# Dividing the rows of one weight matrix among the DMA engines in another way

## The chip, the cores and the metric

The kernel runs on one core of a Trainium2 chip. A core has five engines that work side by side and meet at semaphores: TensorE (PE, matmuls into PSUM; PEld are its weight loads), VectorE (DVE), ScalarE (ACT), GpSimd (POOL) and SyncE (SP), which here issues most of the transfers. Sixteen DMA engines move data between HBM and SBUF, whose 128 partitions are the rows of every tile. The metric is the device time of one execution in microseconds, lower is better.

## What is computed

One decode step for four sequences: an attention block with a KV cache and a gMLP block, both on the same layer-normed input, and their sum with the input itself.

```
def _A_ref(x, k_cache, v_cache, wq, wo):          # B=4, H=32, Sk=4096, Dh=128, D=640
    q = (x @ wq) -> [B, H, 1, Dh]
    p = softmax(q . k_cache * Dh ** -0.5)
    return (p . v_cache) -> [B, 1, H * Dh] @ wo

def _B_ref(x, w_in, w_sp, b_sp, w_out):           # F=1728, Fh=864
    z = gelu(x @ w_in)
    z1, z2 = z[..., :Fh], layernorm(z[..., Fh:])
    g = w_sp * z2 + b_sp
    return (z1 * g) @ w_out

xn = layernorm(x)
out = x + _A_ref(xn, ...) + _B_ref(xn, ...)
```

The K and V caches are 134 MB each in bf16, nearly all of the 282 MB that the kernel reads. The matrix of this study, `w_out`, has 864 rows of 640 values, 1,280 bytes a row, 1.1 MB.

## The kernel before

**Order of the work.** SP's queue loads `wq`, `w_in`, most of `w_out`, and then K and V units in the order of `seq`: four K units, then V unit, K unit in turn. A unit is 8 heads of one sequence, 8.4 MB, 65,536 bytes in each partition. `place` gives each unit two of the five slots of the SBUF tile `kv`; a unit is loaded by `load_unit` (L181) when what lay in its slots has been used. After the last V unit `load_wo` (L189) loads the last three quarters of `wo`, the very last one in five pieces. Meanwhile DVE transposes the K units (L425), PE makes scores (L436) and weighted sums of V (L509), and at the end PE projects with `wo` (L552) and the result goes out (L617, L620).

**The gMLP** lies at the start, while K unit 0 is loaded. The 864 values of z are laid out in SBUF as chunks of up to 128, one value a partition, so that each chunk can be multiplied with as many rows of `w_out`, one row a partition. There are FC = FA + FR chunks: FA = 3 full ones, whose rows lie in `w_out` (in `kv`), and FR more that use only some partitions, whose rows lie in `w_rest`, a view of `w_words`. Partitions that hold no row there are zero (the memset at L128). The matmuls of L338, L339 and L343 make z, ACT applies GELU (L349, L357, L360), POOL and DVE do the layer norm and the gate on 32 x FC wide tiles (L371 to L390), and L403 multiplies with `w_out`, two matmuls a chunk, into `proj`. `w_words` later takes the transposed K units, so L425 can start after L403.

**How `w_out` is divided.** The first 384 rows go to all 128 partitions, three rows each, by SP's queue (L126, L127). The other 480 rows go by the three pieces of `PC`. An entry (p0, p1, n, k) says: partitions p0 to p1, n rows in each, and the source seen as k blocks of rows (`load_piece`, L133), so that k DMA engines move it, one block each. In the trace the first piece has landings on five engines and the second on three of these five. Both go by SP's queue, the third by GpSimd's, on two other engines. `walk` (L141) is a small load by GpSimd's queue on seven engines ahead of the third piece; its data is not used, and the third piece is issued after it.

```
PC = ((0, 20, 10, 5), (32, 44, 12, 3), (60, 68, 17, 2))
return eng.dma_start(out=w_rest[p0:p1, 0:n].rearrange("p c n -> p (c n)"),
                     in_=B_w_out[f_at[t]:f_at[t + 1], :].rearrange("(r i c) n -> i r (c n)", i=k, c=n))
```

So the five engines of the first piece move 4 partitions of 10 rows each, the three of the second 4 partitions of 12 rows, the two of the third 4 partitions of 17 rows.

**Semaphores of transfers.** The transfers of SP's and ACT's queues use eight semaphores in turn. A transfer whose semaphore was used before waits until that earlier transfer has landed, besides waiting for its data and its place.

Of the kernel before, what the change touches and what calls it, by code (L numbers as in the profile page):

```python
# [16 lines left out]
def kernel(  # L17
# [19 lines left out]
    nc = tc.nc  # L37
    P = 128
# [3 lines left out]
    DC = D // P  # L42
# [9 lines left out]
    NG = H // HG  # L52
# [2 lines left out]
    F2 = B_w_in.shape[1]  # L55
    Fh = F2 // 2
    FA = 3
    FR = 17
    nf = FA * P

    PC = ((0, 20, 10, 5), (32, 44, 12, 3), (60, 68, 17, 2))
    f_at = [nf]
    for p0, p1, n, _ in PC:
        f_at.append(f_at[-1] + (p1 - p0) * n)
    assert Fh == f_at[-1]
    FC = FA + FR
    NOUT = A_wo.shape[1]
# [18 lines left out]
    def misc_ps(shape, dtype):  # L86
        misc_ctr[0] += 1
        return ps_m.tile(shape, dtype, tag="misc", name=f"misc{misc_ctr[0]}")
# [5 lines left out]
    n_p = (2 * TC + 1) * 16  # L94
    w_words = const.tile([P, max(2 * NKT + n_p, FR * NOUT // 2)], F32, name="w_words")
    kT_t = w_words[:, 0:2 * NKT].rearrange("p (i n) -> p i n", i=2)
    pT_t = w_words[:, 2 * NKT:2 * NKT + n_p].bitcast(BF16).rearrange("p (j r) -> p j r", r=32)

    def at_slot(i, n, off=0):
        return kv[:, i * SL + off:i * SL + off + n]  # L100
# [22 lines left out]

    w_out = at_slot(2, FA * NOUT, n_in).rearrange("p (c n) -> p c n", c=FA)

    nc.sync.dma_start(out=w_out[:, 0:2], in_=B_w_out[0:2 * P, :].rearrange("(p c) n -> p c n", p=P))  # L126
    nc.sync.dma_start(out=w_out[:, 2:3], in_=B_w_out[2 * P:nf, :].rearrange("(p c) n -> p c n", p=P))  # L127
    nc.vector.memset(w_words[:, 0:FR * NOUT // 2], 0.0)  # L128
    w_rest = w_words[:, 0:FR * NOUT // 2].bitcast(BF16).rearrange("p (c n) -> p c n", c=FR)

    def load_piece(eng, t):
        p0, p1, n, k = PC[t]
        return eng.dma_start(out=w_rest[p0:p1, 0:n].rearrange("p c n -> p (c n)"),  # L133
                             in_=B_w_out[f_at[t]:f_at[t + 1], :].rearrange("(r i c) n -> i r (c n)", i=k, c=n))
# [39 lines left out]
    def load_unit(item):  # L174
        key, u = item
        g, b = divmod(u, B)
        cache = A_k_cache if key == "k" else A_v_cache
        src = cache[b, g * HG:(g + 1) * HG].rearrange("e (m t) d -> (e m) (t d)", t=T)
        c = cuts.get(item, (0, T))
        for t0, t1 in zip(c[:-1], c[1:]):  # L180
            nc.sync.dma_start(out=unit(item, t0, t1), in_=src[:, t0 * Dh:t1 * Dh])  # L181
# [5 lines left out]
    def load_wo(g, c_cuts=(0, HG)):  # L187
        for c0, c1 in zip(c_cuts[:-1], c_cuts[1:]):
            nc.sync.dma_start(out=wo_t[g][:, c0:c1, :], in_=wo_q[g][:, c0:c1, :])  # L189
# [30 lines left out]
    xnT = const.tile([P, DC, 32], BF16)  # L220
# [43 lines left out]
    for q in range(4):  # L264
        nc.gpsimd.tensor_copy(out=SelE[32 * q:32 * q + 32, :, q % 2, :],
                              in_=b8[32 * q:32 * q + 32, 8:8 + HP, None].to_broadcast((32, HP, P // HG)))
# [10 lines left out]
                          in_=ident_f[:].rearrange("p (q x c) -> p q x c", q=2, c=C2))  # L277
# [12 lines left out]
    for hf in range(NH):  # L290
        nc.tensor.matmul(proj[0:32, 0:NO2], lhsT=ident_bf[:XR, 1 - hf:33 - hf],
                         rhs=x_bf[:, hf * NO2:(hf + 1) * NO2], start=(hf == 0), stop=False)
# [4 lines left out]
    for hf in range(2):  # L297
        for c in range(DC):
            for j in range(NG):
                n0 = j * HG * Dh + hf * 512  # L300
                nc.tensor.matmul(q4_ps[32 * j:32 * j + 32, hf * 512:hf * 512 + 512], lhsT=xnT[:, c, :],  # L301
                                 rhs=wq[:, c, n0:n0 + 512], start=(c == 0), stop=(c == DC - 1))
# [14 lines left out]
    w_z = w_in.rearrange("p c (a f) -> p c a f", a=2)  # L317
    z_ps = misc_ps([P, 2, FA, 32], F32)
# [3 lines left out]
    z_in = [[], [], [], []]  # L322
    for t, (p0, p1, n, k) in enumerate(PC):
        src = w_z[:, :, :, f_at[t]:f_at[t + 1]]
        for q in range(p0 // 32, (p1 - 1) // 32 + 1):
# [5 lines left out]
                src_q = src  # L331
            z_in[q].append((t, x0 - 32 * q, x1 - 32 * q, src_q))
    z_of = [[sum((x1 - x0) * PC[t][2] for t, x0, x1, _ in z[:m]) for m in range(len(z) + 1)] for z in z_in]
    w_z2 = w_z[:, :, :, 0:2 * P].rearrange("p c a (q j i) -> p c q a i j", q=4, j=32)
    w_z1 = w_z[:, :, :, 2 * P:nf].rearrange("p c a (q j) -> p c q a j", q=4)
    for c in range(DC):
        for q in range(4):
            nc.tensor.matmul(z_ps[32 * q:32 * q + 32, :, 0:2], lhsT=xnT[:, c, :], rhs=w_z2[:, c, q], start=(c == 0), stop=False)  # L338
            nc.tensor.matmul(z_ps[32 * q:32 * q + 32, :, 2], lhsT=xnT[:, c, :], rhs=w_z1[:, c, q], start=False,  # L339
                             stop=(c == DC - 1))  # L340
        for q in range(4):
            for m, (_, _, _, src) in enumerate(z_in[q]):
                nc.tensor.matmul(zr_ps[32 * q:32 * q + 32, :, z_of[q][m]:z_of[q][m + 1]], lhsT=xnT[:, c, :], rhs=src[:, c],  # L343
                                 start=(c == 0 and m == 0), stop=(c == DC - 1 and m == len(z_in[q]) - 1))
# [5 lines left out]
    for q in range(4):  # L350
        rows = slice(32 * q, 32 * q + 32)
        for m, (t, x0, x1, _) in enumerate(z_in[q]):
            p0, p1, n, k = PC[t]
            z = zr_ps[rows, :, z_of[q][m]:z_of[q][m + 1]]
# [3 lines left out]
            else:  # L358
                for a in range(2):
                    nc.scalar.activation(out=dst[:, a].rearrange("p c (i r) -> p c i r", i=k),  # L360
                                         in_=z[:, a].rearrange("p (r i c) -> p c i r", i=k, c=n), func=ACT.Gelu_apprx_tanh)
# [36 lines left out]
    for f0 in range(0, FC, 4):  # L398
        for hf in range(NH):
            for fc in range(f0, min(f0 + 4, FC)):  # L400
# [3 lines left out]
                                 rhs=(w_out[:, fc] if fc < FA else w_rest[:, fc - FA])[:, hf * NO2:(hf + 1) * NO2],  # L404
                                 start=(fc == 1 and hf == 0), stop=False)
# [11 lines left out]
    def emit_K(u, k):  # L417

        g, b = divmod(u, B)
        hh = first.get(u, 0) ^ (k // 4)  # L420
        qp, kh = k // 2 % 2, k % 2
        t0 = 2 * TC * (2 * hh + qp)
        kw = unit(("k", u), t0, t0 + 2 * TC).bitcast(F32).rearrange("p (t w) -> p t w", w=KW)[:, :, 32 * kh:32 * kh + 32]
        kT = kT_t[:, k % 2]
        nc.vector.transpose(kT.rearrange("p (t r) -> p t r", r=32), kw)  # L425
        if ("S", g) not in state:
            S_new = ps_s.tile([P, 2, TC, M], F32, tag="S", name="S")
            state[("S", g)] = S_new
        S_ps = state[("S", g)]
        kb = kT.bitcast(BF16).rearrange("p (i t e m w) -> p i t e m w", i=2, e=NE, m=M, w=2)  # L430
        w0 = 8 - (b * C2 + hh)
        for w in range(2):
            for i in range(2):
                for e in range(NE):
                    q = 2 * qp + e
                    nc.tensor.matmul(S_ps[32 * q:32 * q + 32, i], lhsT=QZ[:, b, 2 * kh + w, e, w0:w0 + 32],  # L436
                                     rhs=kb[:, i, :, e, :, w], start=(b == 0 and k < 4 and kh == 0 and w == 0),
                                     stop=(b == B - 1 and k >= 4 and kh == 1 and w == 1))
# [89 lines left out]
    def emit_sel(g):  # L528

        ox = misc_ps([P, B, P // HG, HG], F32)  # L530
        nc.tensor.matmul(ox[:].rearrange("p b q c -> p (b q c)"), lhsT=SelX[:].rearrange("p h q -> p (h q)"),  # L531
                         rhs=state["R"][:].rearrange("p b d -> p (b d)"), start=True, stop=True)
        om = ppool.tile([P, B, P // HG, HG], F32, tag="p", name="om")
        nc.vector.tensor_tensor(out=om[:], in0=ox[:], in1=MkQ[:, None, :, None].to_broadcast((P, B, P // HG, HG)), op=ALU.mult)
        state[("om", g)] = om
# [19 lines left out]
    def emit_proj(g, h2=range(2), close=False):  # L555
        for h in h2:
            for hf in range(NH):
                for c in range(4 * h, 4 * h + 4):
                    o_mul(proj[32 * (c % 2):32 * (c % 2) + 32], g, c, hf, hf * NO2, (hf + 1) * NO2, False,
                          close and c == HG - 1 and hf == NH - 1)  # L560

    fill_qz(0)
    for i, item in enumerate(seq):
        if i + 1 < len(seq):
            key, u = seq[i + 1]
            load_unit(seq[i + 1])
            if key == "k" and u == 2 * B - 1:
                load_wo(u // B - 1)
        else:
            load_wo(NG - 3)  # L570
            load_wo(NG - 2)
            load_wo(NG - 1, (0, 2, 4, 6, 7, 8))
        key, u = item
        g, b = divmod(u, B)
        if key == "k":
            done = b == B - 1 and g > 0
            for k in range(8):
                emit_K(u, k)
                if done and k == 1:
                    emit_sel(g - 1)  # L580
                if done and k == 2:
                    emit_oT(g - 1)
                if done and k == 5 and g == 1:
                    emit_proj(g - 1)
            if b == B - 1:
                if g < NG - 1:
                    fill_qz(g + 1)
                softmax(g)
        else:
            emit_V(u)  # L590
# [58 lines left out]
```

## Time and profile before

| | us |
|---|---|
| median of 3 runs | 663.35 (663.31 to 664.25) |
| profiled execution | 663.36 |
| its span, first to last instruction | 661.6 |
| PE, DVE, ACT, POOL busy | 281.7, 377.3, 73.9, 70.3 |
| HBM read | 282.25 MB, 427 GB/s over the span |
| `w_in` landed | 23.89 |
| gMLP: last matmul of L403 ends | about 43.9 |
| K unit 0 landed, first transpose starts | 45.52, 45.74 |
| last piece of `wo` landed | 658.46 |

The profile's page gives each engine's busy time, the span in 40 slices with the share of the DMA engines that is busy, the chain of work that ended last, and groups of instructions with what they waited for. The chain is read backwards from the last instruction; "DMA kv<-in_A_k_cache_dram" in it is time in which the next step waited for that transfer. A line such as "SPq L181 <- X: 9.6, 1, 9.6" says that SP's queue at L181 waited 9.6 us in total for X, once, 9.6 us at the longest. Besides the page, the trace has every DMA packet with its start, duration and size, and the events by which transfers raise their semaphores.

### The profile page before, as it was taken

To read this page: it belongs to the slowest core of one execution; us is meant where nothing else is said; L and a number is where in the kernel's file an instruction comes from. 1 tells how busy PE (TensorE), PEld (TensorE's weight loads), DVE (VectorE), ACT (ScalarE), POOL (GpSimd) and SP (SyncE) were. 2 spreads that over 40 slices of the span, in tenths; PEclk is the share of its full clock that TensorE was granted. 3 is DMA by queue.
4 is the path that set the end of the run, shared out by engine and by line. 5 is a ranking of instruction groups with operands and counts; after the bars stand their busy time and mean duration, and the time that the engine had idled before them with its cause. 6 is when DMAs were issued, how large, how long until landed. Compare 5 with 4: busy or idle time off the path is not lost.

```text
span 661.6 us, 5513 instructions
## 1 busy us (share of the span) xinstructions
PE 281.7 (43%) x2293; PEld 106.9 (16%) x2293; DVE 377.3 (57%) x307; ACT 73.9 (11%) x143; POOL 70.3 (11%) x138
## 2 busy tenths in 40 slices
PE   0445555437052455334435075532606245652236
PEld 0221111112011121111112021110202112120012
DVE  4329989766191758718346196864629175971112
ACT  0300000330100000340200000070110000043200
POOL 3620000030200000130300000030020000003300
PEclk9868879778687697677759677875867778666779
DMA  8999999999999999999999999999999999999997
GB/s 367 458 421 440 425 436 445 436 421 440 421 436 437 444 405 436 441 441 436 433 420 428 437 422 445 442 425 432 432 433 432 433 440 411 446 432 429 423 423 286
DMA packets 7276, 282.60 MB, mean 427 GB/s; under 512 B 929, under 2 KB 1324, under 8 KB 1836
## 3 DMA queue, kind: packets, MB, share of 16 engines
q1 hardware_dynamic: 7112, 282.07, 98.9%
q8 instruction: 18, 0.29, 0.2%
q0 software_dynamic: 112, 0.18, 0.1%
q14 instruction: 6, 0.05, 0.0%
q10 hardware_dynamic: 28, 0.01, 0.0%
HBM read 282.25 MB, written 0.01 MB: 427 GB/s over the span
## 4 chain that ended last, share of the span: by engine, by line
DMA 74%; DVE 12%; issue 11%; PE 2%; ACT 0%; SPq 0%; DVEq 0%; ACTq 0%
DMA kv<-in_A_k_cache_dram 63%; DVE w_words L425 11%; DMA kv<-in_A_v_cache_dram 5%; DMA kv<-in_A_wo_dram 3%; DMA kv<-in_A_wq_dram 3%; PE O L509 1%; DVE w_words L491 0%; PE S L436 0%; DVE Zb L469 0%; DVE m L443 0%; PE last L552 0%; ACT p_bf L485 0%; SPq L189 0%; PE proj L552 0%; PE misc L447 0%
## 5 line engine op out<-in xcount | busy, mean ns | idle before, releaser
L425 DVE STREAM_TRANSPOSE w_words<-kv 128x2048 f32<-128x2048 f32 x128 | 282.8, 2275 | 127.2 <-DMA kv<-in_A_k_cache_dram 127.2
L436 PE MATMUL S<-w_words,QZ 128*32 128x512 bf16 x1024 | 183.3, 490 | 262.5 <-DVE w_words L425 262.5
L436 PEld LDWEIGHTS <-QZ 128*32 128x32 bf16 x1024 | 59.2, 110 | 384.3 <-issue 318.1
L509 PE MATMUL O<-kv,Zb 128*32 128x512 bf16 x1024 | 72.0, 443 | 57.6 <-DMA kv<-in_A_v_cache_dram 51.1
L473 ACT ACTIVATE Zb<-w_words,MkE 32x128 bf16<-32x128 bf16 x120 | 60.9, 508 | 117.2 <-PE O L509 103.3
L518 DVE TENSOR_TENSOR om<-O,Mk 128x512 f32<-128x512 f32 x15 | 10.4, 692 | 92.1 <-PE O L509 92.1
L471 POOL TENSOR_SCALAR Zb<-w_words,MkE 32x128 bf16<-32x128 bf16 x60 | 43.3, 722 | 138.6 <-PE O L509 118.0
L485 ACT ACTIVATE p_bf<-S,negmax 128x1024 bf16<-128x1024 f32 x4 | 4.5, 1114 | 401.5 <-DVE negmax L453 401.5
L509 PEld LDWEIGHTS <-Zb 128*32 128x32 bf16 x1024 | 33.3, 110 | 96.1 <-issue 66.5
L469 DVE TENSOR_SCALAR Zb<-w_words,MkE 32x128 bf16<-32x128 bf16 x76 | 24.9, 327 | 2.3
L411 POOL COPY QZ<-qT 32x32 bf16<-32x32 bf16 x16 | 5.0, 315 | 184.9 <-PE S L436 184.3
L519 DVE TENSOR_REDUCE R<-om 128x128 f32<-128x512 f32 x15 | 15.3, 1020 | 0.5
L496 POOL TENSOR_SCALAR rs<-MkB,rowsum 128x4 f32<-128x4 f32 x4 | 1.2, 296 | 112.2 <-ACT p_bf L485 112.2
L491 DVE STREAM_TRANSPOSE w_words<-p_bf 128x1024 bf16<-128x1024 bf16 (+1 forms) x8 | 9.6, 1240 | 5.9 <-ACT p_bf L485 4.1
L542 POOL MEMSET oT<- 128x66 bf16 x4 | 0.5, 146 | 98.0 <-PE proj L552 98.0
L443 DVE TENSOR_REDUCE m<-S 128x1 f32<-128x1024 f32 x4 | 4.9, 1224 | 6.1 <-PE S L436 6.1
L521 DVE TENSOR_SCALAR R<-O,Mk 128x128 f32<-128x128 f32 x1 | 0.4, 351 | 13.0 <-PE O L509 13.0
L531 PE MATMUL misc<-R,SelX 128*128 128x512 f32 x8 | 4.5, 644 | 7.2 <-DVE R L519 5.5
L301 PE MATMUL q<-kv,xnT 128*32 128x512 bf16 x40 | 4.5, 631 | 6.4 <-DVE xnT L222 6.4
L498 PE MATMUL misc<-rs,SelE 128*128 128x4 f32 x8 | 2.3, 364 | 10.4 <-POOL rs L496 10.4
L552 PE MATMUL proj<-kv,oT 128*8 128x320 bf16 x52 | 5.6, 352 | 1.2 <-DMA kv<-in_A_wo_dram 1.2
L128 DVE MEMSET w_words<- 128x5440 f32 x1 | 4.6, 4592 | 1.9 <-issue 1.9
(107 smaller groups left out, 87.9 us busy)
## 6 DMA issues: line engine op xcount, KB each, us to landing
kv<-in_A_k_cache_dram SPq DMA_DIRECT2D x8, 4096.0 KB, 30.2
kv<-in_A_v_cache_dram SPq DMA_DIRECT2D x1, 6144.0 KB, 28.6
kv<-in_A_wq_dram SPq DMA_DIRECT2D x1, 5120.0 KB, 17.2
kv<-in_A_wo_dram SPq DMA_DIRECT2D x3, 1280.0 KB
kv<-in_B_w_in_dram SPq DMA_DIRECT2D x1, 2160.0 KB, 22.7
kv<-in_A_v_cache_dram SPq DMA_DIRECT2D x1, 2048.0 KB
kv<-in_A_wo_dram SPq DMA_DIRECT2D x3, 320.0 KB, 22.7
kv<-in_B_w_out_dram SPq DMA_DIRECT2D x1, 320.0 KB, 23.0
```

The costliest lines, as they stand in the source:

```text
L411: nc.gpsimd.tensor_copy(out=QZ[r0:r0 + 32, :, :, :, 8 + 8 * hp], in_=qT[32 * g:32 * g + 32, NE * hp:NE * hp + NE].rearrange("p e a b -> p ...
L425: nc.vector.transpose(kT.rearrange("p (t r) -> p t r", r=32), kw)
L436: nc.tensor.matmul(S_ps[32 * q:32 * q + 32, i], lhsT=QZ[:, b, 2 * kh + w, e, w0:w0 + 32], rhs=kb[:, i, :, e, :, w], start=(b == 0 and k < ...
L443: nc.vector.tensor_reduce(out=m1[:], in_=S_ps[:].rearrange("p i t m -> p (i t m)"), axis=AX.X, op=ALU.max)
L469: nc.vector.tensor_scalar(out=dst, in0=src, scalar1=mk, scalar2=None, op0=ALU.mult)
L471: nc.gpsimd.tensor_scalar(out=dst, in0=src, scalar1=mk, scalar2=None, op0=ALU.mult)
L473: nc.scalar.activation(out=dst, in_=src, func=ACT.Copy, scale=mk)
L491: nc.vector.transpose(pT_t[:, j0:j1, :], blocks)
L509: nc.tensor.matmul(O_ps[32 * q:32 * q + 32, :, :], lhsT=Zb[b % 2][:, w].rearrange("p h c -> p (h c)"), rhs=vv[:, w * 4 * Dh:(w + 1) * 4 * ...
L518: nc.vector.tensor_tensor(out=om4[:], in0=O_ps[:], in1=Mk4[:, :, None].to_broadcast((P, 4, Dh)), op=ALU.mult)
L519: nc.vector.tensor_reduce(out=R, in_=om4[:].rearrange("p c d -> p d c"), axis=AX.X, op=ALU.add)
L552: nc.tensor.matmul(dst[0:nb, 0:n1 - n0], lhsT=state[("oT", g)][:, c0:c0 + nb], rhs=wo_t[g][:, c, n0:n1], start=start, stop=stop)
```

## The change

The three pieces get other shapes: 25 partitions of 6 rows on five engines, 15 partitions of 10 rows on three, 12 partitions of 15 rows on two by GpSimd's queue. An engine of the first piece moves 30 rows (40 before), one of the second 50 (48), one of the third 90 (68), and each engine 24 of the first 384 as before. The longest piece has 15 rows a partition instead of 17, so there are 18 chunks instead of 20. The first 384 rows are loaded by one transfer instead of two, with three neighbouring rows of the matrix in each partition, and the matmuls that make z for these chunks become one instead of two for each step. The third quarter of `wo` is loaded in two halves. So there is one transfer fewer ahead of the K units and one more at the end.

```diff
--- before.py
+++ after.py
@@ -55,10 +55,10 @@
     F2 = B_w_in.shape[1]
     Fh = F2 // 2
     FA = 3
-    FR = 17
+    FR = 15
     nf = FA * P
 
-    PC = ((0, 20, 10, 5), (32, 44, 12, 3), (60, 68, 17, 2))
+    PC = ((0, 25, 6, 5), (32, 47, 10, 3), (58, 70, 15, 2))
     f_at = [nf]
     for p0, p1, n, _ in PC:
         f_at.append(f_at[-1] + (p1 - p0) * n)
@@ -123,8 +123,7 @@
 
     w_out = at_slot(2, FA * NOUT, n_in).rearrange("p (c n) -> p c n", c=FA)
 
-    nc.sync.dma_start(out=w_out[:, 0:2], in_=B_w_out[0:2 * P, :].rearrange("(p c) n -> p c n", p=P))
-    nc.sync.dma_start(out=w_out[:, 2:3], in_=B_w_out[2 * P:nf, :].rearrange("(p c) n -> p c n", p=P))
+    nc.sync.dma_start(out=w_out, in_=B_w_out[0:nf, :].rearrange("(p c) n -> p c n", p=P))
     nc.vector.memset(w_words[:, 0:FR * NOUT // 2], 0.0)
     w_rest = w_words[:, 0:FR * NOUT // 2].bitcast(BF16).rearrange("p (c n) -> p c n", c=FR)
 
@@ -331,13 +330,10 @@
                 src_q = src
             z_in[q].append((t, x0 - 32 * q, x1 - 32 * q, src_q))
     z_of = [[sum((x1 - x0) * PC[t][2] for t, x0, x1, _ in z[:m]) for m in range(len(z) + 1)] for z in z_in]
-    w_z2 = w_z[:, :, :, 0:2 * P].rearrange("p c a (q j i) -> p c q a i j", q=4, j=32)
-    w_z1 = w_z[:, :, :, 2 * P:nf].rearrange("p c a (q j) -> p c q a j", q=4)
+    w_za = w_z[:, :, :, 0:nf].rearrange("p c a (q j i) -> p c q a i j", q=4, j=32)
     for c in range(DC):
         for q in range(4):
-            nc.tensor.matmul(z_ps[32 * q:32 * q + 32, :, 0:2], lhsT=xnT[:, c, :], rhs=w_z2[:, c, q], start=(c == 0), stop=False)
-            nc.tensor.matmul(z_ps[32 * q:32 * q + 32, :, 2], lhsT=xnT[:, c, :], rhs=w_z1[:, c, q], start=False,
-                             stop=(c == DC - 1))
+            nc.tensor.matmul(z_ps[32 * q:32 * q + 32], lhsT=xnT[:, c, :], rhs=w_za[:, c, q], start=(c == 0), stop=(c == DC - 1))
         for q in range(4):
             for m, (_, _, _, src) in enumerate(z_in[q]):
                 nc.tensor.matmul(zr_ps[32 * q:32 * q + 32, :, z_of[q][m]:z_of[q][m + 1]], lhsT=xnT[:, c, :], rhs=src[:, c],
@@ -568,7 +564,7 @@
                 load_wo(u // B - 1)
         else:
             load_wo(NG - 3)
-            load_wo(NG - 2)
+            load_wo(NG - 2, (0, 4, 8))
             load_wo(NG - 1, (0, 2, 4, 6, 7, 8))
         key, u = item
         g, b = divmod(u, B)
```

## The prediction

> **What bounds the kernel now.** I read the chain of waits first, then the DMA share by stage, the queue's own waits, and the last stretch.
>
> ```profile
> ## 4 chain that ended last, share of the span: by engine, by line
> DMA 74%; DVE 12%; issue 11%; PE 2%; ACT 0%; SPq 0%; DVEq 0%; ACTq 0%
> ```
>
> Three quarters of the chain is data on its way. The table by stage (columns: stretch, length, busy time of each engine, granted clock, DMA share, GB/s) says how full the way is:
>
> ```profile
> 18.00:46.00 28.00, 11.94 (x143) 6.44 (x144) 5.41 (x11) 6.59 (x13) 14.24 (x35) 0.76 1.04 445
> 46.00:300.00 254.00, 113.59 (x858) 41.83 (x857) 173.04 (x130) 28.79 (x56) 19.72 (x34) 0.78 1.00 433
> 300.00:600.00 300.00, 133.90 (x1036) 48.64 (x1036) 180.71 (x140) 31.86 (x62) 22.34 (x35) 0.73 1.00 432
> 652.00:659.00 7.00, 5.20 (x62) 2.73 (x61) 3.23 (x7) 0.00 (x0) 0.00 (x0) 1.00 0.67 261
> ```
>
> From 18 to 600 us the sixteen DMA engines are full, so the time is what the slowest of them has to move; DVE, the busiest engine, works 173 of 254 us. Only the end is not full:
>
> ```profile
> DMA  9798989999998899999965333433210000000000
> ```
>
> Forty slices of 0.2 us from 652 us: from 656 us on the share falls to a third, and for 2.4 us a few engines still run alone. The chain of that stretch:
>
> ```profile
> 633.82 23.04 DMA kv<-in_A_wo_dram
> ...
> 658.46 0.04 issue
> 658.50 0.32 PE last L552 x4
> 658.82 0.02 issue
> 658.85 0.32 DVE o_bf L617
> ```
>
> The last piece of wo lands at 658.46, four matmuls and one addition follow, and the output. From there 3.11 us to the end of the span (661.57) are fixed. The profiled execution took 663.36 (span plus 1.79), 0.01 from the median of 663.35.
>
> Each transfer on all engines raises its semaphore sixteen times, once per engine; the trace has those events. For wo's last piece they are 654.91; nine from 656.34 to 657.06; 658.02, 658.03, 658.23, 658.27, 658.41, 658.46. Their mean is 657.2, so perfect balance would be worth 1.3 us. Between two K or V transfers every engine needs the same 19.34 us, so an engine keeps its lag, and can be followed from the start to the end. The two engines that get GpSimd's piece land K unit 0 at 44.22 and 44.37 and wo's last piece at 656.92 and 657.06. The three that get both SP pieces land unit 0 last, at 45.10 to 45.52, and end at 658.02 or 658.03, 658.23 and 658.41. Of the two with the first piece alone one ends at 656.34, the other at 658.46. Nine have no piece: eight of these are delayed by 1.5 us each time PE's instructions are fetched (18 fetches of 16,384 bytes, in turn), the ninth never, and ends at 654.91.
>
> **The change, part by part.** *Rows by engine.* Packet durations are the trace's. First piece: 4 packets of 12,800 bytes an engine (479 ns, 1.92 us) become 5 of 7,680 (290 ns, between 102 ns for 2,560 bytes and 388 for 10,240), 1.45: -0.47 on five engines. Second: 4 of 15,360 (573 ns, 2.29) become 5 of 12,800 (2.40): +0.10 on three. GpSimd's: 4 of 21,760 (808 ns, 3.23) become 6 of 19,200 (714 ns, between 644 for 17,280 and 808), 4.28: +1.05 on two. The first three rows per partition in one transfer: 8 x (102 + 55) become 8 x 150 ns; wo's third load in two halves: 8 x 388 become 16 x 197. That is -0.05 and +0.05 on every engine, nothing together.
>
> If nothing else happens, the pair ends at 657.06 + 1.05 = 658.11, the three at 658.04 or before, the others at 658.02 at most: the last landing moves from 658.46 to 658.11, -0.35.
>
> *Where the rows are written.* Before, every engine wrote whole groups of four partitions: 0-3, 4-7 and so on to 16-19, then 32-35 to 40-43, and 60-63, 64-67. None of the 40 packets was longer than its size asks for, nor was any of the 128 w_in packets beside GpSimd's (644 to 647 ns). Now the blocks are of five and six: 0-4, 5-9, 10-14, 15-19, 20-24; 32-36, 37-41, 42-46; 58-63, 64-69. [...] The nearest row for two streams on one path is an instruction fetch beside a K packet: the fetch lasts 0.98 to 1.10 us where a 16,384-byte load lasts 0.61, and the K packet 2.89 where it lasts 2.42. Each loses nearly the other's time while they share. So a strange packet lasts twice as long: pair 2 x 0.714 = +1.43 each, third engine and its host 3 x 0.479 = +1.44, fifth 5 x 0.29 = +1.45. Bounds: 0 and, at one third of the path instead of half, twice these. The row at the lower end: x's four packets and walk's seven, which also write one or two partitions an engine, took 55 and 46 ns, as their size asks for, and the wq packets beside them 1,514 to 1,516. [...] I take the half.
>
> [...]
>
> Sum with meetings: pair 657.06 + 1.05 + 1.43 = 659.54; the third of the three 658.41 - 0.37 + 1.44 = 659.48 at most; the fourth or fifth 658.46 - 0.47 + 1.44 = 659.43. Three separate groups come out within 0.1 us of each other. The last landing moves by +1.08, the profiled time to 663.36 + 1.08 = 664.44.
>
> *The waits.*
>
> ```profile
> SPq L181 <- DMA kv<-in_A_wq_dram: 9.6, 1, 9.6
> ```
>
> K unit 0 is issued at 17.95, after a wait for wq, because it reuses wq's semaphore. One transfer fewer ahead of it shifts the eight semaphores, and it waits for a two-byte load instead; it and nothing ahead of it moves to about 9 us. I cost that at nothing: the engines without pieces land the last w_out rows at 21.24 to 21.6 and K unit 0 19.35 us later, which is eight packets of 2.42, so none was idle. At the end there is one transfer more: the last two pieces of wo now wait for the two parts of the last V unit (landed at 644.18 and 649.06), and are issued by 649.5 instead of 644.19. Behind them in SP's queue is only the output (659.19). The first engine reaches the last piece at about 654.5, and wq's first packets came 1.0 to 2.4 us after its issue: 2.6 us of cover stay. The wo halves let eight of sixteen projection matmuls (655.31, 1.25 us) start some 1.6 us sooner; they end before 656.86 as it is, so nothing.
>
> *The gMLP.* 18 chunks instead of 20, 24 matmuls fewer, vectors of 576 instead of 640; DVE's memset ahead of the pieces (4.59 us) is 0.54 shorter, and they are issued that much sooner, onto engines that are busy with wq. All of it lies between w_in's landing (23.89, which becomes 24.9 or 26.4 on the pair) and the last projection matmul at 43.9; K unit 0 lands at 45.52. It saves about 1.3 us of its 20. Should it end later than K, DVE starts later, but K and V loads are issued 10 us and more before their first packets, so the DMA engines don't notice. The last instruction fetch (655.92) comes 48 instructions later, after its engine's last piece: it frees an engine that isn't the last.
>
> **The rivals.** *No meeting:* the sum without it, 663.36 - 0.35 = 663.0. For it speak the eleven small packets, against it that every line is full and leaves no room. *An uneven meeting, slower:* if the strange packets of the pair get less than half, the pair decides alone: the time is 663.01 plus its loss, so slower by 0.2% (664.68) from a loss of 1.67 us on, and at one third of the path 2.86, 665.9. The fetch rows speak for halves, but there one engine changes between two queues, while here two engines push. *Pair elsewhere:* if the twelve rows of GpSimd's piece went to two engines that take fetches, these would end at about 656.8 + 4.28, 2.6 us late: 666. Against it: walk, which sets where the pair lies, is unchanged. *Hidden anyway:* if the last stretch took up a shift, 663.3; but the last landing is followed at once by the matmuls that need it.
>
> **How the numbers follow.** Even meeting 0.55 at 664.4 (664.1 to 664.8: which of the equal engines is which); uneven 0.17; pair elsewhere 0.03; no meeting or hidden 0.25 at 663.0 to 663.3. A difference of 0.2% (1.33 us) is about what this kernel's measurement tells from none; the three runs differ by 0.94. Of the even meeting about a fifth lies beyond 664.68: slower 0.11 + 0.17 + 0.03 = 0.31; faster, below 662.02, would need all of the 1.3 us that perfect balance is worth: 0.02; same 0.67. The range runs from 662.8 to 665.3, leaving out a part of the uneven cases and pair elsewhere.
>
> **What would show it.** Right: packets of 7,680, 12,800 and 19,200 bytes twice as long where the block leaves its group (up to 0.6, 1.0 and 1.4 us), longer w_in, wq or K packets beside them, and the last landing near 659.5, with the pair among the last. Wrong: all at 290, 479 and 714 ns, and the last landing near 658.1. K unit 0 issued at 9 us, the last wo piece at 649, with no idle DMA before it. The forecast fails if the pair's engines aren't followed rightly from unit 0 to the end, or if the path is shared in another way.

## The result and the profile after

The changed kernel takes 665.11 us in the median (664.90 to 665.36, 13 runs) against 663.35 (663.18 to 664.34, 13 runs) on the same chip: a ratio of 1.0023 with a 95% interval of 1.0016 to 1.0030. It is slower by about 1.76 us, just beyond the 0.2% that I took as the limit of what can be told; the forecast was 664.4. The profiled execution took 665.02, its span is 663.2. The runs of the kernel before fall into two groups, near 663.3 and near 664.3 (4 of 13 here lie in the upper one, 10 of the 19 beside e11 and e12), and no trace was taken of the upper group, so a median or a shift that differs by less than about 1 us has to be read with care.

The chain of waits by engine, and its last pieces (start, length, what):

```profile
## 4 chain that ended last, share of the span: by engine, by line
DMA 74%; issue 12%; DVE 11%; PE 2%; ACT 0%; DVEq 0%; SPq 0%; POOL 0%
```

```profile
617.90 32.87 DMA kv<-in_A_v_cache_dram
650.77 0.02 issue
650.79 9.34 DMA kv<-in_A_wo_dram
660.13 0.04 issue
660.17 0.32 PE last L548 x4
660.49 0.02 issue
660.51 0.32 DVE o_bf L613
```

The end has the same shape as before: the last piece of `wo` lands, four matmuls, one addition, the output. Only the landing is later, 660.13 instead of 658.46, +1.67. The chain now goes through the last V unit instead of an earlier `wo` piece, because the last pieces wait for it and are issued at 650.79. That isn't what makes them late, as the table by stage and the slices of 0.2 us from 652 us on show:

```profile
18.00:46.00 28.00, 11.84 (x119) 6.55 (x120) 4.86 (x9) 6.59 (x13) 13.54 (x34) 0.70 1.02 422
46.00:300.00 254.00, 122.90 (x858) 43.34 (x857) 173.16 (x130) 28.81 (x56) 19.66 (x34) 0.73 1.00 432
300.00:600.00 300.00, 137.35 (x1036) 49.40 (x1037) 180.14 (x140) 30.20 (x59) 20.74 (x33) 0.71 1.00 433
652.00:659.00 7.00, 4.21 (x44) 2.23 (x45) 3.78 (x8) 0.00 (x0) 0.00 (x0) 1.00 0.88 348
```

```profile
DMA  9798989999999999999998999887665443222230
```

From 46 to 600 us the rate is what it was (432 and 433 GB/s; before 433 and 432). From 18 to 46 us it is 422 where it was 445, with the DMA engines as busy as before (share 1.02 after, 1.04 before). The bytes are the same, so 23 of 445 GB/s over 28 us are 1.45 us of every engine. The slices show no gap at the issue of the last pieces; the fall of the share that began at 656 us begins at about 657.4.

Per engine, from the events by which a transfer raises its semaphore sixteen times: K unit 0 landed at 40.60 to 45.52 before (mean 42.52) and lands at 41.64 to 47.42 (mean 43.87), +1.35 on the mean. The last piece of `wo` landed at 654.91 to 658.46 (mean 657.16) and lands at 655.75 to 660.13 (mean 658.68), +1.52. So nearly all of the loss is there when unit 0 has landed, and it isn't that of a few engines: even the earliest landing of unit 0 comes 1.04 us later, and taken in order each of the sixteen comes at least 0.7 us later.

The packets between 10 and 27 us name the place. Of the 7,680-byte packets, nominally 0.29 us, one engine has 0.59, 0.64, 0.63; of the 12,800-byte ones (0.48) one engine has 0.91 and 0.99; GpSimd's of 19,200 (0.71) reach 0.97 and 1.01, and between them the same stretch has `wq` packets of 1.81 to 2.05 (1.51) and `w_in` packets up to 1.27 (0.64). Two K packets last 3.76 and 3.60 instead of 2.42. All this was expected where a block leaves its group of four. Not expected: the K packets of the other engines too last 2.86 at 21 us, and fall back to 2.42 only by 27 us.

### The profile page after: what moved, and what is told of

Read it like the earlier page. It is cut to its first block, busy times and chain, and to the rows that moved or that the text cites. A ratio compares the mean times of both kernels' runs of the same rounds, so it can differ in the third digit from the quotient of the medians.

```text
span 663.2 us, 5465 instructions
## 1 busy us (share of the span) xinstructions
PE 294.2 (44%) x2269; PEld 109.2 (16%) x2269; DVE 376.6 (57%) x307; ACT 73.9 (11%) x143; POOL 69.5 (10%) x138
## 4 chain that ended last, share of the span: by engine, by line
DMA 74%; issue 12%; DVE 11%; PE 2%; ACT 0%; DVEq 0%; SPq 0%; POOL 0%
DMA kv<-in_A_k_cache_dram 61%; DVE w_words L421 11%; DMA kv<-in_A_v_cache_dram 9%; DMA kv<-in_A_wq_dram 3%; DMA kv<-in_A_wo_dram 1%; PE O L505 1%; PE q L300 1%; PE S L432 0%; DVE kv L309 0%; DVE kv L308 0%; ACT kv L308 0%; DVEq L421 0%; SPq L180 0%; PE last L548 0%; DVE o_bf L613 0%
## 5 line engine op out<-in xcount | busy, mean ns | idle before, releaser
L432 PE MATMUL S<-w_words,QZ 128*32 128x512 bf16 x1024 | 193.6, 512 | 250.8 <-DVE w_words L421 250.8
L432 PEld LDWEIGHTS <-QZ 128*32 128x32 bf16 x1024 | 61.1, 112 | 380.7 <-issue 319.4
L505 PE MATMUL O<-kv,Zb 128*32 128x512 bf16 x1024 | 74.9, 457 | 56.4 <-DMA kv<-in_A_v_cache_dram 49.7
L530 DVE TENSOR_TENSOR om<-misc,h 128x512 f32<-128x512 f32 x4 | 2.8, 692 | 4.9 <-PE misc L527 4.9
```

The lines of the kernel that those rows point to most:

```text
L505: nc.tensor.matmul(O_ps[32 * q:32 * q + 32, :, :], lhsT=Zb[b % 2][:, w].rearrange("p h c -> p (h c)"), rhs=vv[:, w * 4 * Dh:(w + 1) * 4 * ...
```

## The experiments

Every version computes the full output. "Meeting" means here, as in the prediction's sum, that an engine writes to a group of four partitions which another engine, its host, loads at the time; an engine that takes part in no meeting is called a bystander. The expectations call such a group a path and number the engines by the blocks of the pieces. Which engine loads which group was my assumption: a packet's record in the trace has a queue, a kind, a start, a duration and a size, and no partitions. The counts of meetings below rest on it; the runs measure what moving or reshaping a piece does. The shifts in the table are against the profile of before (first, mean and last of the sixteen landings); the ratios are against runs of the kernel before on the same chip.

| run | edit | median us | ratio (95%) | K unit 0, first | K unit 0, mean | last landing of wo |
|---|---|---|---|---|---|---|
| after | whole change | 665.11 | 1.0023 (1.0016 to 1.0030) | +1.04 | +1.35 | +1.67 |
| e1 | all but pieces and wo halves | 663.39 | 0.9997 (0.9989 to 1.0006) | -0.12 | -0.17 | +0.07 |
| e2 | pieces alone | 665.01 | 1.0024 (1.0015 to 1.0033) | +1.33 | +1.43 | +1.39 |
| e4 | wo halves alone | 663.48 | 1.0002 (0.9993 to 1.0011) | +0.16 | +0.01 | +0.46 |
| e7 | GpSimd's piece alone | 664.16 | 1.0007 (0.9997 to 1.0017) | +0.98 | +0.80 | +0.74 |
| e8 | blocks of five in SP's pieces | 665.23 | 1.0025 (1.0016 to 1.0035) | +0.86 | +0.99 | +1.66 |
| e10 | blocks of five in the first alone | 663.85 | 1.0005 (0.9996 to 1.0015) | +0.57 | +0.69 | +0.49 |
| e5 | second piece, one meeting | 665.57 | 1.0027 (1.0016 to 1.0038) | 0.00 | +0.15 | +1.97 |
| e9 | second piece, two meetings | 665.73 | 1.0032 (1.0021 to 1.0043) | +2.32 | +2.29 | +2.37 |
| e3 | second piece, three meetings | 665.85 | 1.0034 (1.0021 to 1.0047) | +2.38 | +2.38 | +2.39 |
| e6 | GpSimd's piece, two meetings | 666.24 | 1.0038 (1.0025 to 1.0051) | +2.40 | +1.84 | +2.90 |
| e11 | first piece, one meeting | 664.24 | 1.0003 (0.9994 to 1.0013) | +0.93 | +0.90 | +1.53 |
| e12 | first piece, two meetings | 665.30 | 1.0021 (1.0012 to 1.0030) | +1.80 | +1.81 | +1.81 |

**Which part of the change costs the time?** Theory: the pieces; rivals: the early issue of K unit 0, the merged load, the `wo` halves. Three runs take the change apart. The first is the changed kernel with the old pieces and `wo` unsplit:

```diff
-    FR = 15
-    PC = ((0, 25, 6, 5), (32, 47, 10, 3), (58, 70, 15, 2))
+    FR = 17
+    PC = ((0, 20, 10, 5), (32, 44, 12, 3), (60, 68, 17, 2))
...
-            load_wo(NG - 2, (0, 4, 8))
+            load_wo(NG - 2)
```

> The kernel after with the pieces of before (20, 12 and 8 partitions, every engine on whole groups of four) and wo's third load whole; what is left of the change is the one load of the first 384 rows, its matmuls, and K unit 0 issued at about 8 us. Theory (paths of four partitions): the whole loss comes from the shapes of the pieces, so this is like before, 663.35 within 0.3, with K packets of 2.42 us at 21 us and all w_in packets at 0.64. Rival (early issue): in the profile after, every engine's K packets take 2.86 us at 21 us, falling to 2.42 at 27 us, untouched engines too, which the paths of three engines don't explain; if that comes from K unit 0 waiting in the queues from 8 us on, or from the one load, it stays here: long K packets at 21 us and 664.2, 0.85 over before.

The second is the kernel before with nothing but the new pieces:

```diff
-    FR = 17
-    PC = ((0, 20, 10, 5), (32, 44, 12, 3), (60, 68, 17, 2))
+    FR = 15
+    PC = ((0, 25, 6, 5), (32, 47, 10, 3), (58, 70, 15, 2))
```

> The kernel before with only the three pieces of the change (25, 15 and 12 partitions, 18 chunks); two loads of the first rows, K unit 0 issued at 18 us, wo's load whole. Theory: as the kernel after, 665.1 within 0.3, with the long packets of the pieces (19,200 bytes up to 1.0 us, 12,800 up to 1.0, 7,680 up to 0.6), and the long K packets of all engines too. Rival (early issue): the long packets of the pieces and of their hosts stay, but the K packets of untouched engines are 2.42 us at 21 us, and the time is 664.3.

The third is the kernel before with only the halves:

```diff
-            load_wo(NG - 2)
+            load_wo(NG - 2, (0, 4, 8))
```

> The kernel before with wo's third load in two halves. Theory: nothing, 663.35 within 0.2: 16 packets of 0.199 us an engine for 8 of 0.388, and the last pieces still issued 3 us before their turn. Rival: the additional transfer at the end takes part of the loss of the change: 663.6 or more.

The stretch from 18 to 46 us in the table by stage (the last number is the rate in GB/s), first e1, then e2, then e4:

```profile
18.00:46.00 28.00, 13.20 (x123) 7.14 (x124) 5.18 (x10) 6.59 (x13) 14.10 (x34) 1.00 1.04 450
```

```profile
18.00:46.00 28.00, 12.30 (x135) 7.23 (x137) 4.86 (x9) 6.59 (x13) 13.54 (x34) 0.71 1.02 422
```

```profile
18.00:46.00 28.00, 11.42 (x143) 6.30 (x144) 5.37 (x11) 6.59 (x13) 14.32 (x35) 0.76 1.03 442
```

e2 has the rate and the time of the whole change; e1, in which K unit 0 is issued at 8.32, and e4 have those of before. Where the wait for `wq` went can be read in SP's waits, before in the prediction at 9.6 us, here in the changed kernel:

```profile
SPq L180 <- DMA kv<-in_A_wq_dram: 11.5, 1, 11.5
SPq L180 <- POOL qT L311: 7.5, 1, 7.5
```

It stands now ahead of K unit 1, which waits for `qT` afterwards anyway and is issued at 27.06. And e4's chain shows that the halves alone make the last pieces wait for the last V part, with no loss that the runs can tell:

```profile
617.52 31.96 DMA kv<-in_A_v_cache_dram
649.48 0.02 issue
649.49 9.43 DMA kv<-in_A_wo_dram
```

So the pieces cost it all.

**Is it the group of four?** If what counts is where an engine writes, the old pieces must be slow too when only their place is moved. Rows, packet sizes and the number of chunks stay as before:

```diff
-    PC = ((0, 20, 10, 5), (32, 44, 12, 3), (60, 68, 17, 2))
+    PC = ((0, 20, 10, 5), (44, 56, 12, 3), (60, 68, 17, 2))
```

> The kernel before with the second piece (12 partitions, 12 rows, three engines) at partitions 44 to 56 instead of 32 to 44: same packets, same engines, whole groups of four, but by the theory the paths of the fourth, fifth and sixth engine. Theory: all twelve packets take about 1.15 us instead of 0.573, three other engines' K packets are longer by as much, five engines end 2.2 us later, last landing 660.7, 665.6. Rival (what costs is a block that isn't a whole group of four, wherever it lies): twelve packets of 0.573 us and 663.35.

```profile
18.00:46.00 28.00, 11.86 (x143) 6.54 (x143) 5.07 (x9) 6.59 (x13) 14.27 (x35) 0.76 1.04 412
```

The place alone makes the kernel slower, to 665.85, near the expected 665.6. But the picture was not the expected one: nine of the twelve packets of the piece rose from 0.573 to 1.09 to 1.21 us, and the K packets of all sixteen engines, not of three hosts, were stretched, to as much as 4.65 us beside 2.42. Unit 0 lands 2.4 us later on the mean.

**How many meetings does that take?** The second piece moved by one group has, by that assumption, one meeting (the third engine writes where the fourth loads; the first and second move one group along in step), by two groups two:

```diff
-    PC = ((0, 20, 10, 5), (32, 44, 12, 3), (60, 68, 17, 2))
+    PC = ((0, 20, 10, 5), (36, 48, 12, 3), (60, 68, 17, 2))
```

> The kernel before with the second piece at partitions 36 to 48: the three engines step on by one path each, two onto paths just left by a neighbour that has stepped on too, so only the third meets an engine that loads K, the fourth. The run with the piece at 44 (three meetings) showed what the theory had not: all sixteen engines' K packets took twice their time, and the first engine ended 2.2 us later too. Theory A (a path slows only the two that share it): four packets of 1.15 us, K packets long on one engine only, the first engine of wo's last piece at 654.9 as before, last landing 660.7, 665.6. Theory B (any meeting of SP's packets holds up all sixteen for its whole length): every engine's K packets long, first engine at 657.1, 665.6. Theory C (all are slowed, in proportion to the number of meetings): first engine at 655.6, last 659.2, 664.1.

```diff
-    PC = ((0, 20, 10, 5), (32, 44, 12, 3), (60, 68, 17, 2))
+    PC = ((0, 20, 10, 5), (40, 52, 12, 3), (60, 68, 17, 2))
```

> The kernel before with the second piece at partitions 40 to 52: two of its three engines meet an engine that loads K, the second the fourth, the third the fifth. One meeting (piece at 36) left all other engines alone, first engine of wo's last piece at 654.87; three (piece at 44) slowed all sixteen to half, first engine at 657.18. Theory (one meeting stays local, from two at once on all engines are held up): K packets of all engines long, first engine between 656 and 657.2, last landing 660.7, 665.5 to 665.9. Rival (only three do it): first engine at 654.9, K packets long on two engines alone, 665.5.

First e5, then e9:

```profile
18.00:46.00 28.00, 11.27 (x143) 6.16 (x136) 5.06 (x9) 6.59 (x13) 14.13 (x34) 0.75 1.03 439
```

```profile
18.00:46.00 28.00, 11.89 (x143) 6.49 (x143) 5.06 (x9) 6.59 (x13) 14.29 (x35) 0.76 1.04 411
```

One meeting is the prediction's picture: three of the twelve packets last 1.06, 1.16 and 1.15 us instead of 0.573, the other nine exactly 0.573, and the first landing of unit 0 is unmoved. The host's two K packets at the time last 4.10 and 2.80 us, and the third engine's first K packet, which follows its last stretched one, 2.72. The end of e5 shows its two late engines as a tail of ones, in the slices from 652 us:

```profile
DMA  7969699999899899998979465553211111111110
```

Two meetings at once are another thing: nine of the twelve packets of the piece last 1.11 to 1.21 us, K packets of eight engines 4.5 to 4.6 and the others' at that time up to 4.4, and unit 0 lands 2.3 us later on all sixteen, within some tenths. A third meeting (e3) adds nothing to that: 412 against 411 GB/s. The tail of e9 is that of before, moved:

```profile
DMA  9998989799979797999999998999999974333332
```

In e9, then, packets of 4.5 us and more stand also on engines that by my count write to their own groups alone. No run here shows what they share with the engines that meet.

**Is it the second piece only?** The same with the first piece, by one group and by two (the fifth, or the fourth and fifth, engine on the sixth's and seventh's path):

```diff
-    PC = ((0, 20, 10, 5), (32, 44, 12, 3), (60, 68, 17, 2))
+    PC = ((4, 24, 10, 5), (32, 44, 12, 3), (60, 68, 17, 2))
```

> The same as the one-path run, but in the first piece: at partitions 4 to 24 the engines move one group along in step, and only the fifth writes where another engine loads, on the sixth's path. If one meeting at a time stays between the two engines: the fifth's 4 packets of 12,800 bytes take about 0.96 us instead of 0.479 and the sixth engine's K packet beside them some 1.9 us longer; K packets of all others stay at 2.42 us and the first engine's last landing at 654.4 to 655.2. Two engines are 1.9 us later, so the last landing is between 658.5 and 660.4 (658.46 + 1.9, if the fifth is the one that lands last before), the time 663.4 to 665.3. If any write outside an engine's own group slows all sixteen: K packets above 3 us on most engines and the first engine above 655.5.

```diff
-    PC = ((0, 20, 10, 5), (32, 44, 12, 3), (60, 68, 17, 2))
+    PC = ((8, 28, 10, 5), (32, 44, 12, 3), (60, 68, 17, 2))
```

> The first piece at partitions 8 to 28: the fourth and fifth engine write on the paths of the sixth and seventh, two meetings at once for 4 packets of 12,800 bytes each. If two meetings at once halve all sixteen, whichever piece makes them: the 20 packets last 0.9 us or more instead of 0.479, K packets of all engines rise to about 4.3 to 4.6 us at 21 us, all sixteen land about 1.9 us later, the first engine at 656.3 to 657.0, the last near 660.4, the time 665.2. If a meeting costs only the engines that meet: long packets on two engines and long K packets on two hosts, the first engine at 654.4 to 655.2, the time 663.4 to 665.3.

First e11, then e12:

```profile
18.00:46.00 28.00, 13.21 (x143) 7.54 (x144) 5.06 (x9) 6.58 (x13) 14.15 (x34) 0.76 1.03 429
```

```profile
18.00:46.00 28.00, 12.17 (x143) 6.92 (x143) 5.05 (x9) 6.59 (x13) 13.96 (x34) 1.00 1.03 415
```

Two meetings do it again: from 22 us on all packets of the piece last 0.96 to 1.02 us instead of 0.479, K packets of 3.9 to 4.3 on nine engines, unit 0 1.8 us later on the mean and none of its sixteen landings, taken in order, less than 1.4, and 665.30 as expected (665.2). e11 answers nothing cleanly. The kernel before has a median of 664.18 beside it (663.24 to 664.82), and the runs of e11 lie between 663.32 and 665.66. In its profile, which took 664.89, eighteen of the twenty packets of the first piece are not stretched at all, while six K packets last 3.2 to 4.1 and the second piece, which lies in its own groups, has five packets of 0.79 to 1.03. K unit 0 is issued at 18.72 there instead of 17.95, since `wq` landed later; some engines were idle before it, about 0.1 us on the mean, so that is a small part of the 0.9 us by which unit 0 lands later. So one meeting does not always stay between two engines, and I can't say on what that depends.

**The change's own pieces, one at a time.** GpSimd's piece as in the change, with the other two in whole groups:

```diff
-    FR = 17
-    PC = ((0, 20, 10, 5), (32, 44, 12, 3), (60, 68, 17, 2))
+    FR = 15
+    PC = ((0, 20, 9, 5), (32, 44, 10, 3), (58, 70, 15, 2))
```

> The kernel before with GpSimd's piece as in the change (58 to 70, 15 rows) and the two others on whole groups (20 partitions of 9 rows, 12 of 10). Rows by engine: the three 76 in place of 88, two 36 in place of 40, the pair 90 as in the change. Theory: only the pair and two hosts meet, the pair sets the end at 659.5: 664.4, last landing 659.5, first engine 654.9 to 655.2, K packets at 21 us all 2.42. If that is right, the pair alone explains 1.05 of the 1.7 us, and the rest is what SP's two pieces do to everybody.

Blocks of five in the two pieces of SP's queue, GpSimd's in whole groups:

```diff
-    FR = 17
-    PC = ((0, 20, 10, 5), (32, 44, 12, 3), (60, 68, 17, 2))
+    FR = 15
+    PC = ((0, 25, 9, 5), (32, 47, 9, 3), (60, 68, 15, 2))
```

> The kernel before with the first two pieces in blocks of five as in the change (25 and 15 partitions, 9 rows each) and GpSimd's on whole groups (60 to 68, 15 rows). Rows: the three 90, two 45, the pair 60. Theory A: third, fourth and fifth engine 1.4 to 2.4 us later, last landing 660.5 at most, nobody else touched, 664.7 to 665.4, first engine 654.9. Theory B or C: all engines lose 0.7 to 1.0 us at 21 to 27 us (in the profile after the first engine lost 0.84), first engine 655.7, K packets of all engines up to 2.9, 664.9 to 665.9.

Blocks of five in the first piece alone, with the same 40 rows an engine as before:

```diff
-    PC = ((0, 20, 10, 5), (32, 44, 12, 3), (60, 68, 17, 2))
+    PC = ((0, 25, 8, 5), (32, 44, 12, 3), (60, 68, 17, 2))
```

> The kernel before with its first piece as 25 partitions of 8 rows instead of 20 of 10: the same 40 rows on each of five engines, in blocks of five partitions. Theory: the first four move from path to path in step and meet nobody, the fifth writes all five of its packets (10,240 bytes, 0.388 us) on the paths of the sixth and seventh: these take 0.75 to 0.8 us, it and the sixth end 1.5 to 1.9 us later, nobody else does, first engine at 654.9. If the fifth is the one that ended at 656.34, the time stays 663.4 to 663.6; if it is the one that ended at 658.46, last landing 660.3, 665.2. Rival (more packets of other sizes, not where they lie): 663.35, all packets 0.388.

e7 came to 664.16, near the 664.4 expected of it (its ratio, 0.9997 to 1.0017, is not clear of noise), but again not by two pairs alone: the first landing of unit 0 is 0.98 later, five K packets at 21 us last 2.8 to 3.1, and the mean has moved by 0.80 where two engines and two hosts at 1.43 each would make 0.36. In e8 four of the fifth engine's 11,520-byte packets (0.43) last 0.55, 0.87, 0.93 and 0.83, the last until 24.74, and two of the third's, from 24.47 us on, 0.81 and 0.97. While the fifth meets alone, seven engines' K packets that start at 21.1 to 21.8 us last 2.42 to 2.46; those of eleven engines that start between 23.5 and 25 us, and so reach into both meetings, last 2.8 to 3.0. In e10 the fifth's 10,240-byte packets (0.39) last 0.46, 0.78, 0.81 and 0.78, one host's K packet 3.89; the other engines' K packets last 2.4 to 2.9 and the second piece's up to 0.82 instead of 0.57. So in these profiles each half of the change's pieces slows bystanders somewhat even without the other, by less than e9 or e12. Of the times, only e8's is clear of noise; e10's interval (0.9996 to 1.0015) holds 1, as e7's does.

**GpSimd's piece on other engines' paths altogether:**

```diff
-    PC = ((0, 20, 10, 5), (32, 44, 12, 3), (60, 68, 17, 2))
+    PC = ((0, 20, 10, 5), (32, 44, 12, 3), (64, 72, 17, 2))
```

> The kernel before with GpSimd's piece at partitions 64 to 72 instead of 60 to 68: same packets, same two engines, whole groups of four, each on the path of the engine after it. Theory A: the eight packets take up to 1.6 us, wq and w_in packets of two host engines are long, the pair's second engine, which is a host too, ends up to 4.2 us later: last landing 661.2, 666.1; first engine 654.9 as before. Theory B (a meeting holds up all engines, whichever queue it comes from): all wq packets long, first engine near 658, 666.5. From the profile after, where one strange packet of GpSimd's queue at 10.6 us left all but one engine's wq packets at 1.514, I expect A's picture here.

The eight packets last 0.89 to 1.70 instead of 0.81 and the kernel 666.24, the slowest of all. Here the meetings take place beside `wq` and `w_in`, and the bystanders lose little in each packet that is stretched: `wq` 1.52 to 1.61 for 1.51, `w_in` mostly 0.66 to 0.71 for 0.64. The rates of 9 to 18 and of 18 to 30 us, in e6:

```profile
9.00:18.00 9.00, 0.69 (x2) 0.20 (x2) 4.86 (x11) 0.29 (x1) 4.46 (x14) 1.00 0.92 373
18.00:30.00 12.00, 6.24 (x92) 3.47 (x92) 1.94 (x2) 0.59 (x1) 7.35 (x28) 1.00 1.01 400
```

In the kernel before these were

```profile
9.00:18.00 9.00, 0.69 (x2) 0.10 (x1) 4.96 (x11) 0.29 (x1) 4.34 (x14) 1.00 0.93 399
18.00:30.00 12.00, 6.16 (x101) 2.94 (x101) 3.20 (x6) 4.81 (x10) 9.14 (x31) 0.99 1.07 453
```

The second of these stretches holds another loss, which the mean share hides. One engine of the pair has its last `wq` packet between its stretched ones, it lasts 2.57 us, and `wq` has landed whole at 21.75 instead of 17.93. K unit 0, which in e6 as in the kernel before waits for `wq`, is issued at 21.77:

```profile
SPq L181 <- DMA kv<-in_A_wq_dram: 13.5, 1, 13.5
```

From 21.4 to 22.9 us up to seven of the sixteen DMA engines have no packet at all. Counted from the packets, that is 0.6 us on the mean of sixteen, a third of the 1.84 by which unit 0 lands later, and more than half of the 2.40 by which its first landing comes later. The first K packets then last up to 3.7 us, though GpSimd's last packet had ended at 22.29; `wq`'s first packets in the kernel before, which also start on idle engines, last up to 2.7 instead of 1.51. So e6 shows that these meetings stretch packets, but its 2.9 us at the end are not the price of the meetings alone.

**What was not tried.** A division that has the change's rows an engine but whole groups of four (24 + 30 rows on five engines, and so on) needs 23 chunks for the pair's 90 rows in four partitions, more than the 17 that `w_words` has room for in the kernel before, and wasn't built. Perfect balance would be worth 1.3 us by the landings of before; no version was found that beats the kernel before by more than can be measured.

## Why the prediction was right in kind and short in size

*What bounds the kernel, and where it is decided:* right. The rate from 46 us on did not move, the loss arose before 46 us and was carried to the last landing, and the end behind it is as long as before.

*The sum by packet sizes without meetings* (-0.35, 663.0): not seen in any run, because the new blocks can't be had without meetings. The durations by size were about right: in the changed kernel the fastest packets of the three sizes last 0.295, 0.482 and 0.714. But most of the others there, also of engines that met nobody, are stretched, the 7,680-byte packets to 0.31 to 0.39 and the 12,800-byte ones to 0.48 to 0.63.

*The meetings:* right that they decide. Shown by e3, e5, e9 and e12, in which nothing but the place of a piece is changed; the no-meeting rival falls, and so does the argument for it from eleven small packets. Its price where one meeting was alone was right too: e5's three packets lost 0.48 to 0.59 each, about as much again as their 0.573, and their engine another 0.30 on its next K packet; its host lost 2.07 (1.68 and 0.38 on two K packets) where three times 0.573 are 1.72.

*The step that failed* is the price of the meetings in the sum, +1.08 on the last landing. It charged every meeting to the two engines that meet: two engines and two hosts at 1.43, two more at 1.44 and two at 1.45, which make 11.5 us, or 0.72 on the mean of sixteen. That a group of four has one engine to itself in the full loads, from which the 2, 3 and 5 packets and the hosts in this sum come, no run shows as such; the runs showed in its place that the same twelve packets of 0.573 us are stretched in three cases when they lie 4 partitions further on (e5: 1.06 to 1.16) and in nine when they lie 8 or 12 further on (e9, e3: 1.09 to 1.21). Measured were +1.35 on the mean at unit 0 and +1.67 on the last landing. So the term had about half of the mean loss and two thirds of the shift at the end. What it left out is that the meetings held up bystanders too: two at once stretched the packets of all sixteen engines, to up to about twice their time while they lasted (e9: K packets up to 4.6 for 2.42), and e7, e10 and e11 show some of it with fewer. In the changed kernel the engines without any piece lose about 1.0 by unit 0, and the pair lands unit 0 at 47.31 and 47.42, 0.6 later than 44.37 + 1.05 + 1.43 allows. That is the missing 0.6 at the end (660.13 against 659.54).

*The forecast of 2 x 0.71 for GpSimd's strange packets:* too much for the packets, too little for the pair. They last up to 1.01, but `wq` and `w_in` packets in the same stretch are stretched as well.

*The waits:* right to cost them at nothing. K unit 0 is issued at 7.66 (forecast about 9), and e1 shows that it is worth nothing. The last pieces of `wo` are issued at 650.79 (forecast 649.5, and the V part before them is later by as much as everything else), with no gap in the slices. The gMLP's last matmul ends at about 46.0, before K unit 0 lands (47.42).

*The uneven meeting:* its place on the slower side was right, its mechanism not. It wanted less than half for the pair, which alone would then decide; e5's three packets lasted about twice their time (1.06 to 1.16 for 0.573), and in the changed kernel the pair ends level with others (the last four landings lie within 0.15 us). *Pair elsewhere* fell: GpSimd's packets sit on two engines as before. *Hidden* fell: the shift of the last landing came out whole.

*The chances:* I put 0.31 on slower by over 0.2%, and the measured ratio, 1.0016 to 1.0030, lies there for the most part. That 665.11 lies within the range, which went to 665.3, is in part luck: the even meeting ended at 664.8, and what reached further was the uneven one, whose mechanism did not occur. The spread that I gave the even meeting (664.1 to 664.8) knew only the question which of the equal engines would be last; a loss common to all engines was not among the cases.

## What to carry to other kernels

When rows are divided among DMA engines to balance them, look first at where each engine writes. Here the same twelve packets, moved by four partitions (e5), lasted 1.06 to 1.16 us instead of 0.573 in three cases, with two K packets at 4.10 and 2.80 instead of 2.42; moved by eight (e9), nine of them lasted 1.11 to 1.21, and K unit 0 landed about 2.3 us later on all sixteen engines. A balance worth 0.35 us on paper lost 1.7 here in that way. If a trace shows a packet longer than its size asks for, look whether the packets of engines that have no part in it are longer too, and price the loss on the mean of all engines rather than on the two that meet. Look also whether a transfer that is issued only after one of the stretched ones has landed comes too late, as K unit 0 did in e6.

## What the runs showed that I had not expected

- Two meetings at once slowed every engine here, also those that by my count write only to their own groups: K packets from 2.42 to 4.6 us in e9 and e3, on nine engines to 3.9 to 4.3 in e12. A third meeting added nothing (412 against 411 GB/s from 18 to 46 us). What it is that all sixteen wait for stays open.
- The bystanders' loss differs with what they are moving: in most stretched `wq` and `w_in` packets it was 3 to 10% (e6), in K packets of 65,536 bytes up to 90% (e9). Whether that is the size, the source or the queue of the meeting piece was not tried.
- One meeting alone stayed between two engines in e5, with no bystander's K packet slowed at 23 us, and in e8 until the second began, but not in e10 and e11. In e10 the engines of blocks of five drift against each other, and short further meetings are possible; that is only argued.
